# FNet mixing and a dropless mixture of experts: where the first two batches are folded, and which way batch 1 takes to its second stage

## The chip, the cores and the metric

The kernel runs on one core of a Trainium2 chip. The metric is the device time of one execution in microseconds; three executions of the kernel before give a median of 1250.8 us. TensorE (PE) multiplies, VectorE (DVE) and ScalarE (ACT) work elementwise, GpSimd (POOL) here mainly issues indirect DMAs, and SyncE (SP) issues most other DMAs. Every engine works through its own instructions in the order of the program; semaphores tie them together.

## The reference

```python
X = np.fft.fft(x, axis=1)          # x: (8, 2496, 256) float32
X = np.fft.fft(X, axis=2)
x = X.real.reshape(19968, 256)
logits = x @ w_gate                # 8 experts
expert_idx = np.argmax(logits, axis=1)
gate_w = softmax(logits)[row, expert_idx]
for e in range(8):                 # rows of expert e
    h = np.maximum(x_e @ w1[e], 0) # 256 -> 1024
    y_e = h @ w2[e]                # 1024 -> 256
out = gate_w[:, None] * y          # rows in their own order
```

All in float32: 8 batches of 2496 tokens are mixed by a two-dimensional Fourier transform, of which the real part is kept, and every token then goes through one of 8 two-layer networks.

## The kernel before, in words

The sequence of 2496 is split as 104 x 24. A batch goes through these steps.

*First stage.* The batch comes in three loads ("thirds", `load`, tile `xq`, three buffers), each with four sequence columns and their mirror images, 8 x 256 numbers per partition. `fold` adds a column to its mirror image (L321), and `fold_d` folds the feature axis: the sum and the difference of a row and the same row read backwards (L310, L311) and a small copy (L312). The last third has a column of its own that goes to `pm0`. `half1` multiplies two folded columns by a wave table (`con["w1"]`, 112 columns, or `wp`, the same 110 columns in another order) into PSUM, and ACT copies the result to `t1` (L336). In the trace these matmuls are `s<-xq,w`.

*Between the stages* the rows have to change partitions. Batch 0 does this inside SBUF: in `first_whole`, each of its 12 columns is sent by a small DMA from `t1` to its place in `t4s` (L375), which works since `wp` has the columns in the order that makes the target regular. For every other batch `first` writes each third's `t1` to the DRAM tensor `Td` (L411), and `regroup` reads it back, transposed, into `t4s` in two DMAs (L423).

*Second stage* (`second`): for each half of the batch, groups of matmuls (`pr`, `p<-table,t4s`) go to `zz`, then for five windows of 128 tokens two matmuls (`p<-table,zz`) give the transformed rows and the router's logits. ACT copies parts (L475, L478, mirror at L454), VectorE makes two sets of rows (L480), and `route` (L486) picks the expert on VectorE, counts ranks by matmuls (`rk`) and gives every row a place. `waiting` holds ten scatters per half; `send` issues the next one as an indirect DMA on the POOL queue (L540, shown under the helper's line L238), for batches after 0 with a copy on ACT and a cast on POOL ahead of it. `plan` (L548) makes the table of blocks from the counts, some 22 tiny VectorE operations per block size.

*Expert blocks* (`experts`): a block of 512, 256 or 128 rows of one expert is fetched from `Xs` (`fetch_rows`, five SP DMAs), its weights are fetched (`fetch_weights`), `turn` transposes the rows on VectorE (L654) and negates the odd half on ACT (L657), and two layers of matmuls follow (`ph`, `py`). Blocks of 512 use seven products in place of eight, for which `Left` forms weight sums in a scratch tile `ws` (L637). The first rounds have two blocks of 256 and four of 128 from batch 0, then four of 256 from batch 1.

The order of the work is written out by hand with generators. Every `yield` is a step; the bottom of the kernel decides how many steps of one part are taken between those of another, and since all engines work in program order, this fixes what stands ahead of what on each of them. `second(0)` is stepped through with the first stage of batch 1 (`early`) woven in by `PLAN` (which step of `second(0)` is followed by how many of `early`). After it, `experts` drives: it yields its amount of work, and `side` (the next batch's second stage, and the first stage of the one after, `mixed`) is stepped in proportion. Ahead of the first block stand 12 empty yields (L854), each of which takes one step of `side`. In the kernel before, `early`'s last steps, the table of batch 0 (`close(0)`) and `mixed(1)` are woven from there.

Batch 1's three loads are issued at the end of `first_whole`; batch 2's are issued as `first` of batch 1 releases buffers, the last of them behind `regroup` of batch 1 (L1006).

Of the kernel before, what the change touches and what calls it, by code (L numbers as in the profile page):

```python
# [188 lines left out]
PLAN = {3: 1, 5: 1, 7: 1, 11: 1, 12: 1, 13: 2, 14: 1, 15: 1, 16: 1}  # L189
# [28 lines left out]
def kernel(ctx: ExitStack, tc, x, w_gate, w1, w2, out):  # L218
# [88 lines left out]
    def fold_d(o, a, n):  # L307

        lo, hi = free(a, 1, [D, n], [1, H - 1]), free(a, D - 1, [D, n], [-1, H - 1])
        vec.tensor_tensor(free(o, 1, [D, n], [1, H - 1]), lo, hi, op=ALU.add)  # L310
        vec.tensor_tensor(free(o, H + 1, [D, n], [1, H - 1]), lo, hi, op=ALU.subtract)  # L311
        vec.tensor_copy(free(o, 0, [D, n], [H, 2]), free(a, 0, [D, n], [H, 2]))  # L312

    def fold(xq, q, pm0):

        a, m = xq[:, 0:4], xq[:, 4:8]
        n = 4
        if q == NQ - 1:
            n = 3
            fold_d(pm0, m[:, 3], 1)  # L320
        vec.tensor_tensor(a[:, 0:n], a[:, 0:n], m[:, 0:n], op=ALU.add)  # L321
        yield
        fold_d(m, a, 4)
        yield

    def half1(b, q, half, pm, pm0, t1):
        ps = pm_.tile([NP, 2, D], F32, tag="m", name="s1")
        for i in range(2):
            s = 4 * q + 2 * half + i
            if s < NS - 1:  # L330
                mm(ps[:, i], con["w1"][:, s], pm[:, 2 * half + i])
                continue
            for k, lo, hi in ((NS - 1, 0, H + 1), (NS + 1, H + 1, D)):
                mm(ps[:, i, lo:hi], con["w1"][:, k], pm0[:, lo:hi], True, False)
                mm(ps[:, i, lo:hi], con["w1"][:, k + 1], pm[:, 3, lo:hi], False, True)
        act.copy(t1[:, 2 * half:2 * half + 2], ps[:])  # L336
# [80 lines left out]

    base = con["cap"]
# [9 lines left out]
    t4s = cp.tile([128, 2 * HALF, D], F32, name="t4s")  # L428
    zz = cp.tile([128, 2, NW * 128], F32, name="zz")
# [118 lines left out]
    def plan(b, size, k, last):  # L548
# [38 lines left out]
        if not last:  # L587

            vec.tensor_scalar(n[:], ex[:], -1.0, float(k), op0=ALU.mult, op1=ALU.add)
            vec.scalar_tensor_tensor(n[:], n[:], 0.0, nb[:], op0=ALU.max, op1=ALU.min)  # L590
            nxt = one("gone", E)
            vec.scalar_tensor_tensor(nxt[:], n[:], float(size), gone[:], op0=ALU.mult, op1=ALU.add)
            gone = nxt
        yield
        tabs[b, size, last] = tab
# [27 lines left out]
    class Left:  # L623


        def __init__(self, w1_sb):
            ws = bp.tile([128, 3, F // 2], F32, tag="ws", name="ws", bufs=2)
            o = [ws[:, k] for k in range(3)]
            a11, a12, a21, a22 = (w1_sb[:, c, k * F // 2:(k + 1) * F // 2] for k in range(2) for c in range(2))
            self.all = a11, a12, o[2], a22, o[0], o[1], a21  # L630
            self.due = deque([(o[0], a21, a22, add), (o[1], o[0], a11, sub), (a21, a11, a21, sub),
                              (o[2], a12, o[1], sub)])
# [167 lines left out]
    def experts(todo):  # L800
# [44 lines left out]
        for k, (b, size, last, at) in enumerate(todo):  # L845
            n, m = size // 128, BIG // size
            if not k:
# [3 lines left out]
                while b not in whole:  # L851
                    yield 0, True
                fetch_some(0)
                for _ in range(12):  # L854
                    yield 0, False
# [144 lines left out]
    def ahead_of(b):  # L1000

        yield from first(b)
        regroup(b, 0)
        regroup(b, 1)
        if b == 1:
            load(b + 1, NQ - 1)  # L1006

    def mixed(b):

        one, two = (ahead_of(b + 1) if b + 1 < B else iter(())), second(b)  # L1010
        for _ in range(3):
            next(one, None)
            yield
        for k, _ in enumerate(two):
            if k % 2 == 0:
                next(one, None)
# [41 lines left out]
    for _ in range(3):  # L1058
        next(early)
    for k, _ in enumerate(second(0)):  # L1060
        for _ in range(PLAN.get(k, 0)):
            next(early, None)
        send()
    work = experts(todo)
    steps = {b: mixed(b) for b in range(1, B)}
    for b in range(1, B):
# [4 lines left out]
        if b == 1:  # L1071
            side = woven(chain(close(0), through(0)), chain(early, side))
# [77 lines left out]
```

## Time and profile before

| | |
|---|---|
| three runs | 1249.64, 1250.80, 1251.31 us; median 1250.8 us |
| profiled execution | 1254.3 us; span from first to last instruction 1252.5 us, mean granted TensorE clock 0.977 |
| busy share | PE 97%, PEld 87%, DVE 63%, ACT 35%, POOL 36% |
| chain that ended last | PE 83%, DVE 8%, DMA 3%, ACT 2%, issue 2% |
| DMA | 248.35 MB, mean 198 GB/s |

A busy share is an average over the whole span. The page also gives it in 40 slices of 31.3 us: TensorE has 7, 7, 6 tenths in the first three and 9 in nearly all others, and the granted TensorE clock is 0.7, 0.7, 0.6 there and 0.9 or more afterwards. All that the diff touches happens in the first 140 us, so the trace is read there, in short stretches. Times below are microseconds from the start of the span.

### The profile page before, as it was taken

The page shows a single profiled execution, that of the slowest core. Times are in us where ns is not written, and L with a number is a line of the kernel's source. Part 1 is how long each engine was busy: PE and PEld are TensorE (multiplying, and loading weights), DVE is VectorE, ACT ScalarE, POOL GpSimd, SP SyncE. Part 2 cuts the span into 40 slices and gives each one's busy share as a digit, 9 for nine tenths or more (in the row PEclk, how much of TensorE's full clock was granted, in tenths as well). Part 3 has the DMA queues.
Part 4 walks back from the last instruction along what each step waited for, and adds up shares of the span by engine and source line. Part 5 has one row for each costly group of instructions (what it writes and reads, how often), then busy time and mean ns, then how long its engine had stood idle before and what let it go on. Part 6 is the DMA issues. An engine that isn't in the chain of part 4 may idle for free.

```text
span 1252.5 us, 22624 instructions
## 1 busy us (share of the span) xinstructions
PE 1209.7 (97%) x7389; PEld 1094.7 (87%) x7389; DVE 786.0 (63%) x1862; ACT 441.7 (35%) x1186; POOL 451.8 (36%) x531
## 2 busy tenths in 40 slices
PE   7769999999999999999999999999999999999997
PEld 5558888888888899889988899889989999999996
DVE  4655334566556787666865588686888884444663
ACT  2433333344443433434343433432332332222222
POOL 0336327155137321571226612571463241111112
PEclk7769999999999999999999999999999999999999
DMA  8579899865648443663337434443436238788887
GB/s 242 179 249 348 284 312 310 227 184 193 169 148 266 120 160 117 195 215 112 102 129 216 142 115 165 135 156 97 130 131 190 94 112 305 269 280 289 284 274 283
DMA packets 163065, 248.35 MB, mean 198 GB/s; under 512 B 118542, under 2 KB 130200, under 8 KB 143473
## 3 DMA queue, kind: packets, MB, share of 16 engines
q1 hardware_dynamic: 145644, 201.79, 50.5%
q0 software_dynamic: 16080, 42.85, 9.5%
q10 hardware_dynamic: 1221, 2.24, 0.5%
q8 instruction: 60, 0.98, 0.3%
q14 instruction: 60, 0.49, 0.1%
HBM read 193.45 MB, written 53.45 MB: 197 GB/s over the span
## 4 chain that ended last, share of the span: by engine, by line
PE 83%; DVE 8%; DMA 3%; ACT 2%; issue 2%; SPq 0%; POOL 0%; POOLq 0%; DVEq 0%; ACTq 0%
PE py L223 24%; PE a L223 12%; PE c L223 11%; PE ph L223 9%; PE b L223 6%; PE p L223 6%; PE d L223 6%; PE e L223 5%; PE s L223 4%; DMA xq<-in_x_dram 2%; DVE xT L654 1%; DVE y L754 1%; DVE hT L709 1%; DVE hT L712 1%; DVE hT L706 1%
## 5 line engine op out<-in xcount | busy, mean ns | idle before, releaser
L238 POOL DMA_INDIRECT out_dram<-y,ro x163 | 162.1, 995 | 627.5 <-ACT y L750 303.4
L223 PE MATMUL py<-w_sb,hT 128*128 128x256 f32 x1504 | 340.8, 380 | 0.4 <-DVE hT L908 0.4
L223 PEld LDWEIGHTS py<-w_sb,hT 128*128 128x128 f32 x1504 | 281.1, 190 | 36.6 <-DVE hT L908 0.8
L238 POOL DMA_INDIRECT Xs<-rows,pi x160 | 161.2, 1008 | 87.3 <-POOL pi L539 41.8
L223 PE MATMUL ph<-xT,w_sb 128*128 128x128 f32 (+1 forms) x896 | 127.7, 300 | 4.7 <-DVE ro L863 4.7
L223 PE MATMUL a<-xT,w_sb 128*128 128x256 f32 (+1 forms) x560 | 130.3, 359 | 0.3 <-DVE xT L654 0.3
L223 PEld LDWEIGHTS ph<-xT,w_sb 128*128 128x128 f32 x896 | 118.8, 193 | 11.1 <-DVE ro L863 5.1
L480 DVE SCALAR_TENSOR_TENSOR rows<-p,zs 128x129 f32<-128x129 f32 x160 | 48.8, 347 | 126.0 <-ACT lg L478 125.4
L223 PEld LDWEIGHTS a<-xT,w_sb 128*128 128x128 f32 x560 | 97.6, 190 | 11.7 <-DVE xT L654 0.9
L657 ACT ACTIVATE xT<-xT 128x256 f32<-128x256 f32 (+1 forms) x94 | 36.5, 388 | 173.3 <-DVE xT L654 131.5
L962 ACT ACTIVATE y<-py,xb 128x256 f32<-128x256 f32 x94 | 44.6, 474 | 139.1 <-PE py L223 138.9
L706 DVE TENSOR_TENSOR hT<-hT,b 128x512 f32<-128x512 f32 x63 | 43.3, 687 | 77.5 <-PE b L223 50.3
L716 ACT ACTIVATE hT<-a 128x512 f32<-128x512 f32 x63 | 37.6, 597 | 150.3 <-PE a L223 145.7
L908 DVE TENSOR_SCALAR hT<-ph 128x512 f32<-128x512 f32 x31 | 21.4, 690 | 104.1 <-PE ph L223 52.3
L539 POOL CAST pi<-due 128x1 int32<-128x1 f32 x140 | 47.3, 338 | 64.9 <-ACT due L538 64.9
L223 PE MATMUL c<-xT,ws 128*128 128x256 f32 (+1 forms) x280 | 66.4, 364 | 0.9 <-DVE hT L712 0.2
L223 PE MATMUL a<-w_sb,hT 128*128 128x128 f32 x528 | 66.0, 276 | 0.0
L223 PE MATMUL b<-xs,ws 128*128 128x256 f32 (+1 forms) x280 | 65.0, 359 | 0.0
L223 PE MATMUL d<-xT,w_sb 128*128 128x256 f32 (+1 forms) x280 | 64.9, 358 | 0.0
L223 PE MATMUL e<-xs,w_sb 128*128 128x256 f32 (+1 forms) x280 | 64.9, 358 | 0.0
L223 PE MATMUL c<-xs,ws 128*128 128x256 f32 (+1 forms) x280 | 64.9, 358 | 0.0
L223 PEld LDWEIGHTS a<-w_sb,hT 128*128 128x128 f32 x528 | 63.1, 192 | 0.7
(163 smaller groups left out, 2123.7 us busy)
## 6 DMA issues: line engine op xcount, KB each, us to landing
w_sb<-in_moe_w_dram SPq DMA_DIRECT2D x132, 1024.0 KB
xq<-in_x_dram SPq DMA_DIRECT2D x23, 896.0 KB
xb<-Xs SPq DMA_DIRECT2D x112, 128.0 KB
Td<-t SPq DMA_DIRECT2D x18, 448.0 KB
t4s<-Td SPq DMA_DIRECT2D x7, 768.0 KB
t4s<-Td SPq DMA_DIRECT2D x7, 640.0 KB
xb<-Xs SPq DMA_DIRECT2D x52, 64.0 KB
xb<-Xs SPq DMA_DIRECT2D x88, 32.0 KB
```

The costliest lines, as they stand in the source:

```text
L223: nc.tensor.matmul(o, lhsT=lhsT, rhs=rhs, start=start, stop=stop, **kw)
L238: return unordered(pool.indirect_dma_start(out=dst, out_offset=bass.IndirectOffsetOnAxis(ap=idx, axis=0), in_=rows, in_offset=None, bounds ...
L480: vec.scalar_tensor_tensor(rows[:, k + m, 0:NY], p3[:, 0:NY], zs[:, 0:1], zs[:, 1:], op0=ALU.add, op1=op)
L539: pool.tensor_copy(idx, due[:])
L654: vec.transpose(free(xT[:], 256 * h, [32, n // 32], [BIG, 2], [1, 32]), free(xb, 512 * h, [64, n // 32], [1, 2], [2, 32]))
L657: act.activation(odd, odd, ACTF.Copy, scale=-1.0)
L706: vec.tensor_tensor(h12, h11, b[:], op=add)
L709: vec.tensor_tensor(h21, h12, d[:], op=add)
L712: vec.tensor_tensor(h22, h21, c[:], op=add)
L716: act.activation(h11, a[:], ACTF.Relu)
L908: vec.tensor_scalar(o, ph[:], 0.0, None, op0=ALU.max)
L962: act.activation(y[:, i % 2], py[:], ACTF.Copy, scale=meta[:, i, 1:2])
```

## The change

Batch 1 gets a first stage of its own (`first_one`). Thirds 0 and 1 are folded on GpSimd, both at once at its first step; third 2 is folded on VectorE in pieces of two columns. It multiplies by `wp` instead of `con["w1"]`, VectorE instead of ACT copies the results out of PSUM, and twelve small SP DMAs bring them to `t4b` inside SBUF, as for batch 0. `t4b` is a view of a new tile `spare`, which `Left` later uses, two halves in turn, in place of its two `ws` buffers. There is no `Td[1]` and no `regroup` for batch 1.

Batch 2 (`first_two`) has all three thirds folded on GpSimd in its first step; its products, ACT copies and the way through `Td` stay. The load of its last third is issued in `experts`, behind the row fetch of the first block. The other batches keep `first`.

The order changes: `PLAN` is a new table; all of `early` is issued before `experts` begins, after the first four steps of `close(0)`; a table counts as known one step earlier (`tabs[...]` ahead of the `yield` in `plan`); 14 empty yields stand ahead of the first block instead of 12; `mixed(1)` takes one step of batch 2's first stage first and no other before step 8 of `second(1)`. In the built program this puts one group of batch 2's first-stage matmuls ahead of block 0's first layer, where there were three, and block 0's first two groups of `ph` stand side by side.

The diff:

```diff
--- before.py
+++ after.py
@@ -186,7 +186,7 @@
 SHARE, EARLY, ROOM = 0.6, 0.7, 1.2
 AHEAD = 12
 WARM = 44
-PLAN = {3: 1, 5: 1, 7: 1, 11: 1, 12: 1, 13: 2, 14: 1, 15: 1, 16: 1}
+PLAN = {7: 2, 11: 1, 12: 2, 13: 2, 14: 1, 15: 1, 16: 1, 17: 1}
 MOST = max(k for now in rounds() for _, k, _ in now)
 
 
@@ -304,36 +304,42 @@
                     in_=x[row:row + NP].rearrange("p (c j d) -> p c j d", c=2, d=D)[:, :, 2 * k:2 * k + 2])
                 yield
 
-    def fold_d(o, a, n):
+    def fold_d(o, a, n, eng=vec):
 
         lo, hi = free(a, 1, [D, n], [1, H - 1]), free(a, D - 1, [D, n], [-1, H - 1])
-        vec.tensor_tensor(free(o, 1, [D, n], [1, H - 1]), lo, hi, op=ALU.add)
-        vec.tensor_tensor(free(o, H + 1, [D, n], [1, H - 1]), lo, hi, op=ALU.subtract)
-        vec.tensor_copy(free(o, 0, [D, n], [H, 2]), free(a, 0, [D, n], [H, 2]))
-
-    def fold(xq, q, pm0):
+        eng.tensor_tensor(free(o, 1, [D, n], [1, H - 1]), lo, hi, op=ALU.add)
+        eng.tensor_tensor(free(o, H + 1, [D, n], [1, H - 1]), lo, hi, op=ALU.subtract)
+        eng.tensor_copy(free(o, 0, [D, n], [H, 2]), free(a, 0, [D, n], [H, 2]))
+
+    def fold(xq, q, pm0, eng=vec):
 
         a, m = xq[:, 0:4], xq[:, 4:8]
         n = 4
         if q == NQ - 1:
             n = 3
-            fold_d(pm0, m[:, 3], 1)
-        vec.tensor_tensor(a[:, 0:n], a[:, 0:n], m[:, 0:n], op=ALU.add)
-        yield
-        fold_d(m, a, 4)
+            fold_d(pm0, m[:, 3], 1, eng)
+        eng.tensor_tensor(a[:, 0:n], a[:, 0:n], m[:, 0:n], op=ALU.add)
+        yield
+        fold_d(m, a, 4, eng)
         yield
 
     def half1(b, q, half, pm, pm0, t1):
         ps = pm_.tile([NP, 2, D], F32, tag="m", name="s1")
+        n = NR if b == 1 else NP
+        col = (lambda s: wp[:, s]) if b == 1 else (lambda s: con["w1"][:, s])
         for i in range(2):
             s = 4 * q + 2 * half + i
+            o = ps[0:n, i]
             if s < NS - 1:
-                mm(ps[:, i], con["w1"][:, s], pm[:, 2 * half + i])
+                mm(o, col(s), pm[:, 2 * half + i])
                 continue
             for k, lo, hi in ((NS - 1, 0, H + 1), (NS + 1, H + 1, D)):
-                mm(ps[:, i, lo:hi], con["w1"][:, k], pm0[:, lo:hi], True, False)
-                mm(ps[:, i, lo:hi], con["w1"][:, k + 1], pm[:, 3, lo:hi], False, True)
-        act.copy(t1[:, 2 * half:2 * half + 2], ps[:])
+                mm(o[:, lo:hi], col(k), pm0[:, lo:hi], True, False)
+                mm(o[:, lo:hi], col(k + 1), pm[:, 3, lo:hi], False, True)
+        if b == 1:
+            vec.tensor_copy(t1[0:n, 2 * half:2 * half + 2], ps[0:n])
+        else:
+            act.copy(t1[0:n, 2 * half:2 * half + 2], ps[0:n])
 
     ahead = {}
 
@@ -415,6 +421,66 @@
             pm = xq[:, 4:8]
             yield
 
+    def first_one():
+
+        pm0 = xp.tile([NA, D], F32, tag="pm0", name="pm0")
+
+        def folds(q, eng=vec):
+            xq = ahead[1, q]
+            a, m = xq[:, 0:4], xq[:, 4:8]
+            n = 4
+            if q == NQ - 1:
+                n = 3
+                fold_d(pm0[:], m[:, 3], 1, eng)
+                yield
+            for lo in (0, 2):
+                eng.tensor_tensor(a[:, lo:min(n, lo + 2)], a[:, lo:min(n, lo + 2)], m[:, lo:min(n, lo + 2)], op=ALU.add)
+                yield
+            for lo in (0, 2):
+                fold_d(m[:, lo:lo + 2], a[:, lo:lo + 2], 2, eng)
+                yield
+
+        def products(q):
+            pm = ahead.pop((1, q))[:, 4:8]
+            t1 = xp.tile([NP, 4, D], F32, tag="t1", name="t1")
+            for half in range(2):
+                half1(1, q, half, pm, pm0, t1)
+                for i in range(2):
+                    s = 4 * q + 2 * half + i
+                    nc.sync.dma_start(out=t4b[s:GP:NS, 0:NG], in_=t1[0:NR, 2 * half + i])
+                if half and q < NQ - 1:
+                    load(2, q)
+                yield
+
+        for q in range(2):
+            for _ in folds(q, pool):
+                pass
+        yield
+        yield from products(0)
+        yield from woven(folds(2), products(1))
+        yield from products(2)
+        for h in range(2):
+            ahead[1, "t4", h] = t4b[:, h * HALF:(h + 1) * HALF]
+
+    def first_two():
+
+        pm0 = xp.tile([NA, D], F32, tag="pm0", name="pm0")
+        pms = []
+        for q in range(NQ):
+            xq = ahead.pop((2, q))
+            for _ in fold(xq, q, pm0[:], pool):
+                pass
+            pms.append(xq[:, 4:8])
+        yield
+        for q in range(NQ):
+            t1 = xp.tile([NP, 4, D], F32, tag="t1", name="t1")
+            half1(2, q, 0, pms[q], pm0, t1)
+            yield
+            half1(2, q, 1, pms[q], pm0, t1)
+            nc.sync.dma_start(out=Td[2][:, 4 * q * D:4 * (q + 1) * D], in_=t1[:].rearrange("p j d -> p (j d)"))
+            load(3, q)
+            yield
+
     base = con["cap"]
 
     def regroup(b, h):
@@ -426,6 +492,9 @@
         ahead[b, "t4", h] = t4
 
     t4s = cp.tile([128, 2 * HALF, D], F32, name="t4s")
+    spare = cp.tile([128, 2, 3, F // 2], F32, name="spare")
+    t4b = spare[:].rearrange("p a b f -> p (a b f)").rearrange("p (g d) -> p g d", d=D)
+    turns = [0]
     zz = cp.tile([128, 2, NW * 128], F32, name="zz")
 
     def second(b):
@@ -591,8 +660,8 @@
             nxt = one("gone", E)
             vec.scalar_tensor_tensor(nxt[:], n[:], float(size), gone[:], op0=ALU.mult, op1=ALU.add)
             gone = nxt
-        yield
         tabs[b, size, last] = tab
+        yield
 
     def fetch_rows(b, size, tab, i, flat=None):
 
@@ -624,7 +693,8 @@
 
 
         def __init__(self, w1_sb):
-            ws = bp.tile([128, 3, F // 2], F32, tag="ws", name="ws", bufs=2)
+            ws = spare[:, turns[0] % 2]
+            turns[0] += 1
             o = [ws[:, k] for k in range(3)]
             a11, a12, a21, a22 = (w1_sb[:, c, k * F // 2:(k + 1) * F // 2] for k in range(2) for c in range(2))
             self.all = a11, a12, o[2], a22, o[0], o[1], a21
@@ -850,8 +920,10 @@
                 fetch_some(0, 1)
                 while b not in whole:
                     yield 0, True
+                fetch_some(0, 1)
+                load(2, NQ - 1)
                 fetch_some(0)
-                for _ in range(12):
+                for _ in range(14):
                     yield 0, False
                 for xT in turn(b, size, xbs[0][0]):
                     pass
@@ -999,20 +1071,21 @@
 
     def ahead_of(b):
 
-        yield from first(b)
+        if b == 1:
+            yield from first_one()
+            return
+        yield from first_two() if b == 2 else first(b)
         regroup(b, 0)
         regroup(b, 1)
-        if b == 1:
-            load(b + 1, NQ - 1)
 
     def mixed(b):
 
         one, two = (ahead_of(b + 1) if b + 1 < B else iter(())), second(b)
-        for _ in range(3):
+        for _ in range(1 if b == 1 else 3):
             next(one, None)
             yield
         for k, _ in enumerate(two):
-            if k % 2 == 0:
+            if k % 2 == 0 and (b > 1 or k > 7):
                 next(one, None)
             yield
         yield from woven(close(b), one)
@@ -1055,12 +1128,16 @@
         else:
             vec.tensor_copy(con["rd"][:, c, to + E:to + 2 * E], pg[:])
     early = ahead_of(1)
-    for _ in range(3):
-        next(early)
+    next(early)
     for k, _ in enumerate(second(0)):
         for _ in range(PLAN.get(k, 0)):
             next(early, None)
         send()
+    closed = close(0)
+    for _ in range(4):
+        next(closed)
+    for _ in early:
+        send()
     work = experts(todo)
     steps = {b: mixed(b) for b in range(1, B)}
     for b in range(1, B):
@@ -1069,7 +1146,7 @@
         side = chain(steps[b], islice(steps.get(b + 1, iter(())), AHEAD))
         ticks = TICKS + AHEAD * (b == 1)
         if b == 1:
-            side = woven(chain(close(0), through(0)), chain(early, side))
+            side = woven(chain(closed, through(0)), side)
         blocks = [(size, k * size / BIG, halved(b - 1, size)) for size, k, _ in rounds()[b - 1]]
         total = sum(k * (15 if seven_ else 16) for _, k, seven_ in blocks)
         open_ = sum(k * (8 if seven_ else 16) for _, k, seven_ in blocks)
```

More of the change, by code (lines that the diff above doesn't have):

```diff
@@ L593, in plan @@
             gone = nxt
+        tabs[b, size, last] = tab
         yield
-        tabs[b, size, last] = tab
     def fetch_rows(b, size, tab, i, flat=None):
```

## The prediction

> **What bounds the kernel now.** I read four views in turn: the busy shares, then the stretches of 5 us for the place where TensorE is idle, then the waits for the reason, then the timeline for the chain behind it. TensorE is 97% busy, so of the span's 1252.5 us only 42.8 are without a matmul, and the slices put most of that ahead of 110 us. Columns below: stretch, length, busy us (and instructions) of PE, PEld, DVE, ACT, POOL, then granted clock, DMA share, GB/s.
>
> ```profile
> 55.00:60.00 5.00, 2.15 (x23) 1.67 (x21) 3.84 (x20) 1.98 (x7) 2.79 (x3) 0.86 0.93 313
> 60.00:65.00 5.00, 0.00 (x0) 0.00 (x0) 4.62 (x23) 0.00 (x0) 3.59 (x3) 0.50 0.61 206
> 65.00:70.00 5.00, 0.43 (x3) 0.47 (x3) 4.66 (x19) 0.00 (x0) 3.78 (x5) 0.50 0.99 314
> 70.00:75.00 5.00, 5.00 (x20) 4.56 (x21) 0.31 (x5) 1.83 (x5) 3.81 (x4) 0.50 1.00 350
> ...
> 80.00:85.00 5.00, 2.83 (x16) 2.12 (x16) 3.69 (x14) 2.63 (x11) 0.00 (x0) 1.00 0.32 68
> 85.00:90.00 5.00, 2.26 (x5) 1.85 (x6) 3.21 (x14) 0.74 (x3) 0.00 (x0) 0.59 0.45 99
> ```
>
> Two holes stand out: 58 to 69.5, and 82 to 87.7. After each the clock is at 0.50 for some microseconds, so work there takes twice as long. The waits up to 120 us name them:
>
> ```profile
> PE pr L223 <- DMA t4s<-Td: 11.2, 1, 11.2
> PE ph L223 <- DVE ro L863: 4.7, 1, 4.7
> ```
> ```profile
> SPq L606 <- DMA Xs<-rows,pi: 12.6, 2, 11.6
> ```
>
> The first is batch 1's trip through DRAM (Td written, read back as t4s). The second is the start of the first expert block, and behind it SyncE waited 11.6 us for batch 0's scattered rows. The timeline gives that chain:
>
> ```profile
> 73.75 0.97 POOL L238 DMA_INDIRECT Xs<-rows,pi  x1 [0.30 <-issue]
> ...
> 81.15 1.96 SPq L606 DMA_DIRECT2D xb<-Xs  x4
> ...
> 86.99 0.70 DVE L654 STREAM_TRANSPOSE xT<-xb 128x512 f32<-128x512 f32 x1
> ...
> 87.74 3.78 PE L223 MATMUL ph<-xT,w_sb 128*128 128x256 f32 x8 [4.68 <-DVE ro L863]
> ...
> 113.14 7.07 PE L223 MATMUL ph<-xT,w_sb 128*128 128x256 f32 x32
> ```
>
> Read it as: last row scatter issued at 73.75, landed 7.4 us later, fetched, transposed, block 0 at 87.74. That, not the hole of 11.2 us, is the clock of the start: a matmul brought forward into the hole helps only if it would otherwise stand behind block 0.
>
> **A yardstick.** In both programs TensorE has the same matmuls ahead of block 1's first layer, which starts at 113.14, and soon after it the instruction orders agree. So I sum to that point.
>
> **The change, part by part.**
>
> *GpSimd folds two thirds of batch 1.* A fold is an add of 1024 elements per partition, an add and a subtract of 508, and a copy. GpSimd's nearest row is the weight differences:
>
> ```profile
> L678 POOL TENSOR_TENSOR ws<-w_sb,ws x26: 1269/1302/1616, 413.6 to 1010.7; 128x512 f32<-128x512 f32 x26
> ```
>
> 512 elements in 1.30 us is 2.54 ns each: 2.6 + 2 x 1.3 + 0.6 for the copies (the casts at L539 are 0.34) gives 6.0 us per third. No row has GpSimd reading backwards as these folds do, so 5.5 to 9 us; I take 6.0. Third 0 lands at 29.3 (there L321 starts), so it is done at 35.3, third 1 at 41.3; the row scatters queued behind them on POOL start at 44.96 today. Hidden, then, up to 7.8 us a third. VectorE loses two folds (1.22 + 0.69 + 0.68 + 0.17 us each) and L321's wait for the second load, about a window of rows earlier; but the two matmul groups and VectorE's copies of them now stand together ahead of the routing (about 3 us).
>
> Here a rule weighs against the change. The trace shows VectorE held by GpSimd:
>
> ```profile
> 410.77 1.46 POOL L678 TENSOR_TENSOR ws<-w_sb 128x512 f32<-128x512 f32 x1
> ```
> ```profile
> 411.13 1.64 DVE L310 TENSOR_TENSOR xq<-xq 104x508 f32<-104x508 f32 x1
> 412.70 0.67 DVE L311 TENSOR_TENSOR xq<-xq 104x508 f32<-104x508 f32 x1
> ```
>
> L310 takes 1.64 us instead of 0.67, ending 0.54 after GpSimd's add. The Trainium skill (SBUF — State Buffer, section Who interferes with whom) generalises: a VectorE instruction with two SBUF inputs is blocked for the whole of a GpSimd instruction that reads SBUF. By the row alone, which shows it on long operands, routing's small operations lose nothing and the one-hot of half 0 is ready at 41.0; by the rule its five two-input operations (L495, L496, L498, L501, L505) each wait 0.3 to 0.5 us and it is ready at 42.8. Today it is 42.04. I take 42.0: no change.
>
> *VectorE copies batch 1's first stage (ACT did).* Half 1 of batch 0 today takes from 42.04 to 60.10 (`base`). VectorE gets four copies at 0.69 (L908, PSUM to SBUF, 128x512) = 2.8 us and the cut-up third 2 (two 0.42 pairs for each 0.68 pair). TensorE paces the middle of this stretch at clock 0.50, so some is covered; what is not: a fold between the last rows and the reduce (1.2) and two copies between the one-hot and `base` (1.4). Price 2.5, `base` at 62.6. If TensorE stays at full clock here it is 3 us less.
>
> *Sends.* Ten scatters follow. Today their nine gaps average 1.44 us; the ones near VectorE's fold of batch 2 are 1.8 to 1.95, the rest 1.28. That fold leaves VectorE: 62.6 + 0.7 + 9 x 1.28 = 74.8 for the last issue, +1.1.
>
> *Batch 1 inside SBUF, third 2 of batch 2 behind the rows.* Td's write and read-back, 1.3 MB each way, become twelve SBUF copies of 110 KB (0.77 us of SyncE each, none of it late: the last pair trails the last VectorE copy as batch 0's do, 4 us from copy to L223's `pr`, so batch 1 resumes at 65 instead of 69.56). A 0.9 MB load goes behind the first rows. What this buys is the landing. Two stretches, 44 to 48 and 71 to 75 us:
>
> ```profile
> Xs<-rows,pi POOLq DMA_INDIRECT x2, 3.2
> ```
> ```profile
> Xs<-rows,pi POOLq DMA_INDIRECT x3, 7.4
> ```
>
> 7.4 us is at a DMA share of 1.00; 3.2 to 7.4 bound it. Only 2 MB of weights now share the way, so 4.0: rows landed at 78.8 (81.15). The fetch moved its last bytes 3.9 us after issue today (the DMA engines fall idle at 85.0), and VectorE's folds hid that until 86.99; now the rows can be transposed at 82.8.
>
> *GpSimd folds all of batch 2.* It starts when the last scatter has been issued, 75.8. Third 0 takes 5.5, and routing of batch 1, at that time on VectorE, costs it 0.9 more: 82.2. In TensorE's order batch 2's first matmul group stands between batch 1's half and block 0: 1.9 us at clock 0.50, 84.1. In ACT's order its copy (0.59) stands ahead of the odd half of xT (0.42): 85.1 against today's 88.14. So block 0 starts 3.0 earlier, bound by GpSimd and no longer by the rows. Thirds 1 and 2 are done at about 88 and 95, needed at about 94 and 101: hidden, 6 us in hand. Batch 1's scatters wait behind them (95 instead of 97.8 by program order: nothing).
>
> *Moved behind block 0.* Today three groups of batch 2's first stage run before block 0, then one: 2 x 0.95 = 1.9 us comes behind it. VectorE's routing, held by the folds, may stop `p` once: 0.4 (0 to 1.5).
>
> *Fourteen ticks, scratch tile moved, table known earlier.* They set the order counted above; no cost of their own. Left's scratch (L637) is first needed at 239 us.
>
> Sum: -3.0 + 1.9 + 0.4 = -0.7 us. The profiled execution has 1254.3 us (1252.5 and 1.8 around it), 3.5 over the median 1250.8; a difference carries over: **1250.1 us**. This kernel's measurement can tell about 0.2% (2.5 us) from no change.
>
> **Rivals.**
>
> *A, likeliest, 0.45: the gain of the landing is paid back* as summed. Own range -3 to +2.
>
> *B, 0.30: faster, 1246.8.* The routing isn't held (one-hot at 41.0) or TensorE keeps its clock in half 1. For it: the stretch from 30 to 35 has clock 0.88, and fewer stalls on VectorE keep TensorE denser; against: 0.50 from 40 on. One of them is 1 to 3 us on the whole chain; with 2 us and a landing of 3.4, rows and folds are ready 2.6 earlier: -0.7 - 2.6 = -3.3, with -4 taken for some of both.
>
> *C, 0.20: slower, 1254.9: GpSimd becomes the bound.* At 9 us a third, batch 1's third 0 is done at 38.3, and VectorE's copy of its product, ahead of the routing in VectorE's queue, moves the one-hot by 2; the last scatter's end is 77.8; the fold of batch 2 ends 9 later at 86.8, plus 1.9 and 1.0: 89.7 against 88.14, +1.6, and 1.9 + 0.6 moved behind: +4.1. It decides from about 8.2 us a third. For it: backward reading, the lock. Against: the rows at 1.30.
>
> *D, 0.05: the trip inside SBUF is no shorter* (twelve small copies land late): batch 1's half stays where it was, routing reaches VectorE at 84 and delays xT; about +0.5, 1251.3.
>
> **How the numbers follow.** A reaches 2.5 us to either side only at its ends (0.03 faster, 0.04 slower). Faster: nearly all of B, 0.29, and A's end: 0.32. Slower: C and A's end, 0.24. Same: 0.44. The range holds B's centre and most of its far side (1246.0, a clock kept through half 1) and C's centre less its tail: 1246.0 to 1254.9.
>
> **What would show it.** Right: `pr` of batch 1 near 65; last scatter issued near 74.8 and landed in 4; the first fold group of batch 2 on POOL ending near 82, ph at 84 to 85, and block 1's first layer 112 to 113. Half 1's clock at 0.50. Wrong: folds on POOL above 8 us a third; `s` or ph waiting for POOL; routing's short operations at 1 us and more; block 1 before 110 or after 116.

## The result, and the profile after

The changed kernel takes 1246.91 us (median of 15 runs, 1244.42 to 1250.88) where the kernel before takes 1250.38 us on the same chip (15 runs, 1248.34 to 1255.59). The ratio is 0.9971, with a 95% interval of 0.9959 to 0.9982: faster by about 3.5 us. The forecast was 1250.1 us and "the gain of the landing is paid back". Two later measurements, on two chips, gave 0.9966 (0.9957 to 0.9974) and 0.9973 (0.9961 to 0.9985). On one more chip, of which more below, nothing of the gain was left.

A caution before the lines are read: the two profiled executions differ by more than the medians. That of the kernel before (1254.3 us) was 3.9 over its median, that of the changed kernel (1244.87 us, span 1243.1) 2.0 under its own.

First the same stretches of 5 us (length, busy us and instructions of PE, PEld, DVE, ACT, POOL, granted clock, DMA share, GB/s), changed kernel:

```profile
45.00:50.00 5.00, 4.97 (x28) 4.06 (x26) 3.44 (x8) 2.11 (x10) 3.88 (x4) 0.90 0.36 110
...
55.00:60.00 5.00, 1.41 (x16) 1.26 (x14) 3.79 (x22) 0.27 (x1) 1.96 (x2) 0.50 0.75 237
60.00:65.00 5.00, 2.24 (x11) 2.27 (x11) 4.35 (x29) 0.53 (x2) 3.91 (x4) 0.50 0.65 216
...
70.00:75.00 5.00, 1.71 (x12) 1.49 (x12) 3.18 (x9) 2.15 (x10) 4.60 (x4) 1.00 0.43 161
75.00:80.00 5.00, 2.72 (x6) 1.66 (x7) 3.18 (x7) 1.00 (x2) 4.92 (x5) 0.68 0.58 136
```

Both holes of TensorE are still there and earlier. The first is shorter. The second is as long as before (4.8 us); a group of batch 2 and 0.7 us more of waiting follow it. The DMA share between 70 and 75 us, where the last rows of batch 0 have to land, is 0.43 instead of 1.00. The waits up to 120 us of the same kernel:

```profile
PE pr L223 <- DVE p_nb L630: 6.3, 1, 6.3
PE s L223 <- POOL xq L312: 4.8, 1, 4.8
PE ph L223 <- DVE xT L724: 0.7, 1, 0.7
```
```profile
SPq L675 <- DMA Xs<-rows,pi: 10.0, 1, 10.0
```

`pr` waits 6.3 us instead of 11.2. The name behind the arrow misleads: `pr` reads nothing of the table of blocks, and other profiles of this kernel name other tiny instructions of that table. In the trace TensorE's queue first goes through the counters of its DMA queues, which hold it until 62.65, and looks at VectorE's last. What it waits for are the last small DMAs into `spare`, issued up to 57.54; the last of their completions is counted at 62.41. In front of block 0 TensorE's wait (4.7 us for `ro` before) now stands at the first group of batch 2, which waits 4.8 us for GpSimd. Then the chain that set the start, in the timeline:

```profile
70.46 0.98 POOL L238 DMA_INDIRECT Xs<-rows,pi  x1 [0.30 <-issue]
...
74.32 2.38 SPq L675 DMA_DIRECT2D xb<-Xs  x4
...
78.40 0.71 DVE L724 STREAM_TRANSPOSE xT<-xb 128x512 f32<-128x512 f32 x1 [1.73 <-DMA xb<-Xs]
...
79.17 5.89 PE L223 MATMUL ph<-xT,w_sb 128*128 128x256 f32 x16 [0.71 <-DVE xT L724]
...
106.12 7.07 PE L223 MATMUL ph<-xT,w_sb 128*128 128x256 f32 x32
```

The last scatter is issued at 70.46 (73.75 before), the fetch starts 3.9 us later (7.4 before), and VectorE waits 1.73 us for the fetched rows: in this profile block 0 hangs on its rows, with nothing of VectorE's in between. (In two later profiles of the same kernel something of VectorE's does stand there; see "GpSimd sets block 0" below.) Block 1 starts at 106.12 instead of 113.14.

### The profile page after: what moved, and what is told of

Same layout as the page of the kernel before. It is cut to its first block, busy times and chain, and to the rows that moved or that the text cites. A ratio compares the mean times of both kernels' runs of the same rounds, so it can differ in the third digit from the quotient of the medians.

```text
span 1243.1 us, 22669 instructions
## 1 busy us (share of the span) xinstructions
PE 1205.0 (97%) x7389; PEld 1092.3 (88%) x7389; DVE 784.7 (63%) x1849; ACT 438.0 (35%) x1180; POOL 475.0 (38%) x562
## 4 chain that ended last, share of the span: by engine, by line
PE 68%; issue 18%; DVE 8%; POOL 3%; ACT 2%; DMA 1%; POOLq 0%; SPq 0%; DVEq 0%; ACTq 0%
PE py L223 20%; PE a L223 10%; PE c L223 9%; PE p L223 6%; PE b L223 5%; PE d L223 5%; PE ph L223 5%; PE e L223 4%; PE s L223 3%; POOL out_dram L238 3%; DVE xT L724 1%; DVE y L824 1%; ACT y L820 1%; DVE hT L776 1%; DVE hT L779 1%
## 5 line engine op out<-in xcount | busy, mean ns | idle before, releaser
L223 PE MATMUL c<-xT,spare 128*128 128x256 f32 (+1 forms) x280 | 66.5, 364 | 0.9
L223 PE MATMUL c<-xs,spare 128*128 128x256 f32 (+1 forms) x280 | 64.9, 358 | 0.0
L223 PE MATMUL b<-xs,spare 128*128 128x256 f32 (+1 forms) x280 | 64.9, 359 | 0.0
```

Of the source, the lines that this page charges most:

```text
L223: nc.tensor.matmul(o, lhsT=lhsT, rhs=rhs, start=start, stop=stop, **kw)
```

## The experiments

### Three parts of the change taken back, one at a time

(The four runs on a second chip, which stand last here, came before these.)

*Batch 1 through DRAM again*, the folds and copies as changed:

```diff
-        n = NR if b == 1 else NP
-        col = (lambda s: wp[:, s]) if b == 1 else (lambda s: con["w1"][:, s])
+        n = NP
+        col = lambda s: con["w1"][:, s]
...
-                    nc.sync.dma_start(out=t4b[s:GP:NS, 0:NG], in_=t1[0:NR, 2 * half + i])
+                if half:
+                    nc.sync.dma_start(out=Td[1][:, 4 * q * D:4 * (q + 1) * D], in_=t1[:].rearrange("p j d -> p (j d)"))
...
-            ahead[1, "t4", h] = t4b[:, h * HALF:(h + 1) * HALF]
+        regroup(1, 0)
+        regroup(1, 1)
```

> Batch 1's first stage goes through DRAM and back as before; the folds on GpSimd, VectorE's copies, the late load and the 14 steps stay. Theory 'landing' (the gain comes from the traffic that no longer stands beside batch 0's last rows): 3 to 4 us over the changed kernel, so level with the kernel before or 1 us over it; the last scatter lands 5 to 7.5 us after its issue instead of 3.9, and batch 1's first resampling product starts at 66 to 70 us instead of 62.8. Theory 'folds' (the gain is VectorE's relief from five folds): within 1 us of the changed kernel, 0.997 of the kernel before.

*Thirds 0 and 1 of batch 1 folded on VectorE again*, the trip inside SBUF and the rest as changed:

```diff
-PLAN = {7: 2, 11: 1, 12: 2, 13: 2, 14: 1, 15: 1, 16: 1, 17: 1}
+PLAN = {3: 1, 7: 2, 11: 1, 12: 2, 13: 2, 14: 1, 15: 1, 16: 1, 17: 1}
...
-            for _ in folds(q, pool):
+            for _ in folds(q):
                 pass
-        yield
+            yield
```

> Thirds 0 and 1 of batch 1 are folded on VectorE, one of them in step 3 of batch 0's second half and one in step 7; the trip inside SBUF, the rest on GpSimd and all else stay. Theory 'landing': within 1 us of the changed kernel in the end; the first routing one-hot comes at 41.5 to 43 us instead of 40.1, and no operation of the first routing is held by GpSimd (0.24 us each instead of 1.2 to 1.5 for three of them). Theory 'folds': 1.5 to 3 us over the changed kernel, the whole of batch 0's rows later by that much. If GpSimd's holding of VectorE costs more than the folds do (three operations by 1.1 us): 1 us under the changed kernel.

*Thirds 0 and 1 of batch 2 folded on VectorE again*:

```diff
-            for _ in fold(xq, q, pm0[:], pool):
+            for _ in fold(xq, q, pm0[:], pool if q == NQ - 1 else vec):
```

> Thirds 0 and 1 of batch 2 are folded on VectorE as before, third 2 on GpSimd; all else as in the changed kernel. Theory 'landing': within 1 us of the changed kernel: the first group of batch 2 starts before 76 us because VectorE folds a third in 2.8 us instead of GpSimd's 5.1, but the rows set the start of block 0 anyway. Theory 'folds': 1.5 to 3 us over the changed kernel, since VectorE has 5.5 us of folds more at the time when it does batch 1's routing and block 0's transposes. Rival C of the prediction (GpSimd is the bound at block 0): 1 to 2 us under the changed kernel.

Beside them, on the same chip, the changed kernel itself:

> The changed kernel itself, beside the three partial undoings, so that all share one chip. On the chip of the prediction it was 0.9971 of the kernel before; on a second chip 1.0009. There TensorE's completion signals came late in bursts (none before 409.04 to 414.60 us, then four within 0.2 us) and TensorE stood idle for 35.6 us after 56 us instead of 14.8. If the size of the gain depends on such stalls, a chip without them (span about 1243 to 1247) gives 0.996 to 0.998, and one with them (span about 1275 to 1280) gives 0.999 to 1.002. If the gain is the same everywhere, 0.9971 again.

| | median us | ratio to the kernel before (95%) |
|---|---|---|
| kernel before | 1251.81 | |
| changed kernel | 1247.11 | 0.9966 (0.9957 to 0.9974) |
| batch 1 through DRAM | 1251.35 | 1.0002 (0.9990 to 1.0014) |
| batch 1 folded on VectorE | 1252.47 | 1.0014 (1.0001 to 1.0026) |
| batch 2 folded on VectorE | 1248.13 | 0.9978 (0.9966 to 0.9989) |

The gain is there again. Taking back the trip inside SBUF gives up 4.2 us, all of the gain within the interval. So far "landing" is right and "folds" wrong. But taking back GpSimd's folds of batch 1 gives up 5.4 us, which is more than the whole change brought and which neither theory allowed: "landing" had put it at under 1 us. Taking back the two folds of batch 2 gives up 1.0 us, with overlapping intervals, so that they are worth anything is not shown; "GpSimd is the bound at block 0" would have made that variant faster.

The profiles say where each loses. With batch 1 through DRAM, the waits from 60 us on:

```profile
PE pr L223 <- DMA t4s<-Td: 13.9, 2, 12.1
PE ph L223 <- DVE ro L934: 4.3, 1, 4.3
```

and in its timeline:

```profile
69.24 0.98 POOL L238 DMA_INDIRECT Xs<-rows,pi  x1 [0.30 <-issue]
...
75.73 1.92 SPq L674 DMA_DIRECT2D xb<-Xs  x4
```

The scatter is out even earlier than in the changed kernel, and the fetch follows 6.5 us later instead of 3.9. The landing is slow again as soon as the traffic of `Td` is back. The direction is clear, the size less so. In this profile landing and fetch take 3.3 us longer than in the mean of the changed kernel's three profiles (table below), but both halves are shorter (half 1 takes 16.5 us instead of 17.6, at a granted clock of 0.90), and counted from the first `pr` block 1 starts only 1.1 us later. The profiled execution lay 1.5 us under its own median. That the trip is worth 4.2 us is shown by the medians; this one profile locates only a part of it.

With batch 1 folded on VectorE, VectorE's own timeline of batch 0's first half reads:

```profile
29.21 1.29 DVE L437 TENSOR_TENSOR xq<-xq 104x512 f32<-104x512 f32 x2 [3.41 <-DMA xq<-in_x_dram]
...
34.33 1.29 DVE L437 TENSOR_TENSOR xq<-xq 104x512 f32<-104x512 f32 x2 [1.83 <-DMA xq<-in_x_dram]
...
37.02 0.61 DVE L549 SCALAR_TENSOR_TENSOR rows<-p,zs 128x129 f32<-128x129 f32 x2
...
42.91 1.28 DVE L340 COPY t<-s 110x512 f32<-110x512 f32 x2
...
45.40 0.24 DVE L570 TENSOR_TENSOR oh<-table,v 128x80 bf16<-128x80 f32 x1
```

VectorE stands still 3.41 and 1.83 us for loads of batch 1, then folds, and batch 0's rows and routing wait behind in its queue; two copies more stand right ahead of the routing. The one-hot comes 19.1 us after batch 0's first `pr` instead of 14.4 to 15.2. The kernel before has the same two waits in the same place, without the copies:

```profile
29.32 1.22 DVE L321 TENSOR_TENSOR xq<-xq 104x1024 f32<-104x1024 f32 x1 [4.67 <-DMA xq<-in_x_dram]
...
33.96 1.23 DVE L321 TENSOR_TENSOR xq<-xq 104x1024 f32<-104x1024 f32 x1 [1.50 <-DMA xq<-in_x_dram]
...
35.10 0.60 DVE L480 SCALAR_TENSOR_TENSOR rows<-p,zs 128x129 f32<-128x129 f32 x2
```

So the parts don't add up one by one: the two losses, 4.2 and 5.4 us, together are twice the gain. With the folds on VectorE, batch 0's first half is 3.5 us longer than in the kernel before (19.1 against 15.9 and 15.3), about what the landing gives. The two copies are 1.3 us of it. Another part comes from the order of this variant: it folds the whole second third in one go, so the next rows start at 37.02, where the kernel before lets them through after the first addition, at 35.10. A variant that folds on VectorE in the old order was not run, so how much of the 5.4 us belongs to GpSimd as such is open. With the folds on GpSimd that half is shorter than before. By the medians, neither of the two parts brought anything here without the other.

### The kernel before once more, and batch 2's trip

> The kernel before, profiled a second time. If the first profile was typical: from batch 0's first resampling product to its first one-hot 16.2 us, to the last scatter's issue 47.9, to block 1 87.3. If the first profile was a late one (it stood 3.9 us over its own median), the last scatter is issued at 45 to 47 us from that product, and block 1 starts at 83 to 86. VectorE's first fold of batch 1 waits some 6 us for the load of third 1, with the routing of half 0 behind it in the queue.

> The changed kernel itself, as the base for the two variants beside it: 0.9966 of the kernel before, give or take 0.001, on a chip on which TensorE's completion signals are not late. Counted from batch 0's first resampling product, so that the loads at the start are left out, its profile has block 0 at 53.5 to 54.5 us and the start of block 1 at 80.5 to 82.5; the wait for batch 2's trip through DRAM in front of its resampling is between 0 and 3 us.

The changed kernel took 1247.01 us beside 1251.03 for the kernel before (0.9973, 0.9961 to 0.9985). The second profile of the kernel before has its last scatter at 46.1 us after the first `pr`, and block 1 at 85.1: so the first one (47.9 and 87.3) was a late one, as its distance from the median said. With two profiles of the kernel before and three of the changed kernel the span can be cut at rows of the timeline, each piece set beside the forecast's term. All are starts of rows: first `pr` of batch 0; `oh` of half 0; `base` of half 1; the tenth scatter of half 1; the first fetch of rows; `ph` of block 0; `ph` of block 1.

| piece | before, us | changed, us | change of the means | forecast |
|---|---|---|---|---|
| start to the first `pr` | 25.9, 26.3 | 25.5, 28.3, 26.0 | +0.5 | 0 |
| half 0, to its one-hot | 15.9, 15.3 | 14.4, 15.2, 14.4 | -0.9 | 0 |
| half 1, to `base` | 18.1, 17.1 | 18.1, 17.3, 17.3 | 0.0 | +2.5 |
| to the last scatter | 13.8, 13.8 | 12.4, 12.4, 12.4 | -1.4 | -1.4 |
| landing, to the fetch | 7.4, 6.8 | 3.9, 4.0, 3.7 | -3.3 | -3.4 |
| fetch to block 0 | 6.6, 6.6 | 4.8, 5.4, 5.7 | -1.3 | -0.7 |
| block 0 to block 1 | 25.4, 25.6 | 27.0, 27.8, 26.2 | +1.5 | +2.3 |
| block 1 to the end | 1139.4, 1139.7 | 1137.0, 1140.7, 1141.2 | +0.1 | 0 |
| sum | 1252.5, 1251.2 | 1243.1, 1251.1, 1246.8 | -4.8 | -0.7 |

-4.8 is near the -3.5, -4.7 and -4.0 by which the medians fell. Of the 4.1 us between the two sums, half 1 alone makes 2.5. The first and the last row show what one profile is worth: they vary by 3 and 4 us without a cause in the change. The landing and the sends stand far outside that; half 0's 0.9 is only just clear of its spread.

In the second and third profile of the changed kernel, and in the variant with batch 2 folded on VectorE, something had come up behind block 1. This is a wait of the latter:

```profile
PE pr L223 <- DMA t4s<-Td: 3.0, 1, 3.0
```

(1.4 and 2.0 us in the two profiles of the changed kernel.) Batch 2 still takes the way through DRAM, and block 1 now comes to it sooner. Two variants bring that trip forward, the first by the order of steps alone, the second with the VectorE folds as well:

```diff
-            if k % 2 == 0 and (b > 1 or k > 7):
+            if (b > 1 and k % 2 == 0) or (b == 1 and (k == 8 or k > 10)):
```

> Batch 2's first stage takes its steps one after another from step 11 of batch 1's half instead of at every second one, so that its last third's products come ahead of block 0's second layer instead of behind it. Theory 'paid back at batch 2's trip' (after block 1 has moved forward, TensorE waits 1.4 us, in a variant 3.0 us, for the read-back of batch 2, and runs at a lower clock after it): the wait goes, and the time falls by 1.5 to 3 us under the changed kernel. Theory 'the wait is chance' (the changed kernel's first profile had none): within 0.7 us. If the earlier trip collides with block 1's rows or its weights: 1 to 2 us slower.

> The same order of steps, and batch 2's thirds 0 and 1 folded on VectorE. By 'paid back at batch 2's trip' this takes away the 3.0 us wait that stood in the profile of the variant with these two folds on VectorE: level with the variant of the steps alone or 1 us under it, 2 to 4 under the changed kernel. If VectorE is the bound around block 0 (routing of batch 1, folds, transposes): 1 to 2 us over the changed kernel.

In both profiles the wait is gone. The times are 1246.05 us (0.9951, 0.9935 to 0.9968, only five runs) and 1247.80 us (0.9972, 0.9963 to 0.9981), beside 1247.01 for the changed kernel. The first may be a microsecond or two better, but its interval overlaps the changed kernel's, and the second, with the same wait removed, is level. Whether batch 2's trip costs anything is therefore open. That the wait exists is shown, that it is worth 1.5 us or more is not.

### Four kernels on a second chip

These came first, and all on one chip that runs this program slower: the kernel before at 1278.39 us.

> The changed kernel itself once more, for a second look and as the base of the three beside it. Its profile had block 1's first layer at 106.1 us (113.1 before), 7.0 us earlier, and the span 9.4 us shorter, while the medians differ by 3.5. If those 7 us belong to the change, block 1 starts at 106 to 107 again and the ratio is 0.997. If a good part is the state of TensorE's clock in half 1 of batch 0 (0.90 between 45 and 50 us there, 0.50 before) and that state falls out by chance, block 1 starts somewhere between 106 and 110, with a lower clock in that stretch when it is late.

> Undoes one part: ScalarE copies batch 1's first-stage results out of PSUM instead of VectorE. By the prediction's price (2.5 us for VectorE's copies between one-hot and base) base of half 1 comes 1.4 to 2.5 us earlier, and with it the scatters and block 0: 1 to 2 us under the changed kernel (1245). Rival: ScalarE's copies (0.59 each, six) delay the small copies that the rows and the routing wait for, base is no earlier or later, 0 to 2 us over.

> Undoes one part: the load of batch 2's last third is issued at the end of batch 1's first stage, ahead of the weights and the rows, as before. Theory of the landing: the last scatters share the DMA engines again and land after about 7 us instead of 3.9, block 0 starts 3 us later, 2 to 3 us over the changed kernel (1249 to 1250). Rival, the load is hidden anyway: landing 4 to 5 us, the same time as the changed kernel within 1 us; or a little faster, since GpSimd's last fold no longer waits for it.

> Adds 96 bfloat16 matmuls of 128x256 whose result nobody reads into TensorE's three waits: 24 ahead of the rank counts of batch 0's half 0, 36 ahead of batch 1's second stage, 36 ahead of batch 2's first group. Clock theory: half 1 of batch 0, batch 1's second stage and block 0's first two groups run at clock 1.00 instead of 0.50; the rank counts to base of half 1 gain up to 2 us, block 0's first groups 2.9: 2 to 4 us under the changed kernel (1243 to 1245). Rival, VectorE and the scatters pace the stretch: only the 1.9 of block 0's first groups, or nothing. If 24 run at half clock they end after the one-hot and cost up to 1 us.

The edits, in the same order (the first is the changed kernel as it is; in the last, `heat` issues bf16 products of constants into PSUM banks that are free then, 96 in three places, and nothing is left out of the computation):

```diff
-            vec.tensor_copy(t1[0:n, 2 * half:2 * half + 2], ps[0:n])
+            act.copy(t1[0:n, 2 * half:2 * half + 2], ps[0:n])
```
```diff
         yield from products(2)
+        load(2, NQ - 1)
         for h in range(2):
...
-                fetch_some(0, 1)
-                load(2, NQ - 1)
                 fetch_some(0)
```
```diff
+        if b == 0 and h == 0:
+            heat(24)
         rk = pm_.tile([128, NSL + 1, E], F32, tag="m", name="rk")
...
+            if b == 1 and h == 0:
+                heat(36)
...
+            if q == 0:
+                heat(36)
             half1(2, q, 0, pms[q], pm0, t1)
```

| | median us | ratio to the kernel before (95%) |
|---|---|---|
| changed kernel | 1279.27 | 1.0009 (0.9989 to 1.0028) |
| ScalarE copies batch 1's first stage | 1280.99 | 1.0017 (0.9994 to 1.0039) |
| batch 2's last third loaded early | 1284.69 | 1.0060 (1.0040 to 1.0081) |
| products in TensorE's waits | 1283.62 | 1.0041 (1.0022 to 1.0061) |

*Copies.* With the copies back on ScalarE, half 1 (one-hot to `base`) takes 20.5 us, as it does with them on VectorE (20.5). Half 0 is 0.9 shorter. No gain came of it in the time. So the forecast's 2.5 us for VectorE's copies in half 1 isn't there. This run tests that term directly, though on this chip alone.

*Load.* Loading batch 2's last third ahead of the rows costs 5.4 us here, more than the 2 to 3 expected; landing and the way from the fetch to the transpose are 1.1 and 2.5 us longer in its profile. In the trace the four row transfers that the transpose needs are complete at 83.5, and it starts at 90.8, straight behind batch 1's routing on VectorE. So the early load's cost is shown for this chip, but only a part of it is the landing.

*Clock.* The time went the other way, 4.4 us over the changed kernel. Three stretches of the kernel with the extra products:

```profile
40.00:45.00 5.00, 4.84 (x42) 4.09 (x40) 3.99 (x19) 2.33 (x9) 1.52 (x2) 1.00 0.81 243
45.00:50.00 5.00, 2.90 (x20) 2.41 (x18) 2.25 (x6) 0.94 (x4) 3.78 (x5) 1.00 0.53 155
50.00:55.00 5.00, 2.05 (x4) 1.06 (x4) 1.36 (x5) 1.24 (x6) 3.78 (x5) 0.50 0.92 271
```

The clocks without them are 0.68, 0.98 and 0.71. Over the whole of half 1 the mean granted clock rose only from 0.71 to 0.76, and half 1 became 21.6 us instead of 20.5. At block 0 the products stand in the way (the transpose starts 3.5 us before `ph` instead of 0.8). What the clock is worth can't be read from this run, since ScalarE stands still for 3.15 us in its half 1, from 47 to 50, for a late signal of the kind that the next paragraph describes. The ten profiles from the other three chips say more. There half 1 takes 18.1, 18.1 and 18.4 us at a mean clock of 0.69, from 16.8 to 17.6 at 0.79 to 0.81 (five profiles), and 16.3 and 16.5 at 0.89 and 0.90. So half 1's length does go with TensorE's clock. Whether the clock shortens half 1, or a half with fewer waits keeps the clock up, no run here separates.

*The chip.* The changed kernel's profile there has TensorE idle for 35.6 us from 56 us on, counting only gaps over 0.4 us, where the first chip has 14.8. Some of this idleness stands where TensorE, VectorE and ScalarE all stand still:

```profile
70.10 0.77 PE L223 MATMUL p<-table,zz 128*128 128x145 f32 x4 [1.47 <-issue]
...
75.42 0.27 ACT L544 COPY zs<-p 128x130 f32<-128x130 f32 x1 [5.37 <-remote]
75.79 0.61 DVE L549 SCALAR_TENSOR_TENSOR rows<-p,zs 128x129 f32<-128x129 f32 x2 [5.94 <-remote]
```

ScalarE needs nothing but this product; it ends at 70.9, and ScalarE starts 4.5 us later. In the trace TensorE's semaphore, which ScalarE waits for, is not counted up between 69.67 and 75.39. From 409.04 to 414.60 us the same happens while five groups of products end, and then four counts come within 0.2 us. Neither the kernel before nor the changed one shows a burst of this kind on the first chip, and no kernel does on the two later ones. In the first of these gaps batch 1's routing stood still, so the rows of block 0, landed in 4.0 us as elsewhere, had their transpose 8.8 us after the start of the fetch instead of 4.1 to 4.9. That is some 4 us at the very place where the change gains. Why the signals are late on that chip is not known, and the kernel before was not profiled there, so it isn't shown that they take just this gain.

## Why the prediction was wrong in its likeliest case

Its range held the time, and its point was 3.2 us too high. Point by point:

*What bounds the start: right in the main.* The chain from the last scatter over landing and fetch to block 0 set the start in all three profiles of the changed kernel on the faster chips; in two of them VectorE's routing added up to 0.9 us behind the landed rows (below). The landing went from 7.1 to 3.9 us (forecast 4.0). Batch 1 through DRAM brought a landing of 6.5 us and the old time back. The sends, 1.28 us apart without VectorE's fold, were right to 0.1.

*"Half 1: price 2.5": the step that failed most.* It charged VectorE 2.8 us of copies and cut-up folds, and counted as covered only what TensorE's slow clock would hide. Here is half 1 before and after, with the same columns as above, and in each VectorE's wait for ScalarE's logits (`lg`) ahead of the rows (ten of them: busy us and mean ns, then the idle time ahead of them):

```profile
42.04:60.10 18.06, 14.34 (x80) 12.35 (x79) 10.57 (x44) 7.59 (x26) 10.70 (x10) 0.69 0.69 208
L480 DVE SCALAR_TENSOR_TENSOR rows<-p,zs 128x129 f32<-128x129 f32 x10 | 3.0, 347 | 6.6 <-ACT lg L478 6.6
```
```profile
40.14:58.20 18.06, 14.16 (x80) 12.28 (x80) 13.05 (x52) 5.22 (x21) 10.43 (x10) 0.69 0.68 204
L549 DVE SCALAR_TENSOR_TENSOR rows<-p,zs 128x129 f32<-128x129 f32 x10 | 3.0, 348 | 3.2 <-ACT lg L547 3.2
```

VectorE did get busier there (10.6 to 13.1 us of 18.1), but it had been idle for 7.5 us of half 1, 6.6 of them in that wait. The added work went into it: the wait fell to 3.2 us, and half 1 kept its length. The clock isn't behind that: it is 0.69 in both, and in the two kernels' profiles with a clock of 0.80 the lengths are 17.1 before and 17.3 after. An engine's added busy time was taken for time on the chain, without looking at what it waited for there.

*"Half 0: no change": sized wrong by 0.9.* The forecast set VectorE's two products' copies against the two folds and the wait for the second load. The lines above show both loads' waits in VectorE's queue, with batch 0's rows behind them. Of the waits it named only the second load's. Without the first one too, batch 0's first rows start 4.4 us after the first `pr` instead of 6.0 (first profiles). How much of the 0.9 us each item makes is not shown. The rule that the forecast weighed here held: the Trainium skill (SBUF — State Buffer, section Who interferes with whom) has VectorE's two-input instruction blocked for a whole GpSimd instruction, and two short ones in the changed kernel show it:

```profile
37.34 0.54 DVE L564 TENSOR_TENSOR eq<-lg,mx 128x80 f32<-128x80 f32 x1
37.92 1.47 DVE L565 TENSOR_TENSOR eq<-eq,table 128x80 f32<-128x80 f32 x1
```

They take 0.24 us each in the kernel before and in the variant whose folds are on VectorE; L565 stays held through two of GpSimd's instructions and ends when GpSimd's last piece of the third does (39.4). In the three profiles this cost 0.8 to 1.5 us in front of the one-hot, less than the 1.8 that lay between the forecast's two sums. The row alone, which said that short operations lose nothing, was wrong, though its figure (41.0) was the nearer one: counted from the same first `pr` as the kernel before, the one-hots are ready at 40.5 to 41.4. Two errors met.

*"GpSimd sets block 0": its own fold was sized too long by 1.3 us, and it delays block 0 by another way.* The forecast had 6.4 us for the fold of batch 2's first third with routing's hold. Here it is in the timeline of the changed kernel, with routing's held instruction among its own:

```profile
71.45 2.36 POOL L321 TENSOR_TENSOR xq<-xq 104x1024 f32<-104x1024 f32 x1
...
73.90 1.26 POOL L310 TENSOR_TENSOR xq<-xq 104x508 f32<-104x508 f32 x1
73.96 1.29 DVE L565 TENSOR_TENSOR eq<-eq,table 128x80 f32<-128x80 f32 x1
...
75.11 1.26 POOL L311 TENSOR_TENSOR xq<-xq 104x508 f32<-104x508 f32 x1
...
76.57 1.89 PE L223 MATMUL s<-xq,w 104*112 104x256 f32 x4 [4.77 <-POOL xq L312]
```

It took 5.1 us. VectorE is held, GpSimd is not. The first group ends just as the transpose of the rows starts (78.4), so here the rows bound block 0, in a near tie. In the other two profiles of the changed kernel it is VectorE. This is the third:

```profile
76.10 2.33 POOL L321 TENSOR_TENSOR xq<-xq 104x1024 f32<-104x1024 f32 x1
```
```profile
76.38 2.08 DVE L567 TENSOR_TENSOR v<-v,table 128x10 f32<-128x10 f32 x1
...
78.68 0.71 DVE L724 STREAM_TRANSPOSE xT<-xb 128x512 f32<-128x512 f32 x1
```

L567, an operation of 10 elements that takes 0.17 us in the kernel before (L498 there), ends only when GpSimd's addition for the second third of batch 2 does, and the transpose stands behind it in VectorE's queue. The trace has the rows complete at 77.8, 0.9 us before the transpose starts; in the second profile L567 takes 2.08 us too, and the transpose starts 0.7 us after the rows are complete. So GpSimd's folds do reach block 0, through routing on VectorE and not through TensorE's group as forecast. With the two folds on VectorE the hold is gone from the profile, and the time was no better.

The price per element (2.3 to 2.5 ns) and the reading backwards were no problem: rival C, from 8.2 us a third, was far off. The forecast's own terms for batch 1's third add up to 5.8 us, not the 6.0 that it took; 5.5 was measured.

*"1.9 and 0.4 come behind block 0": near*, 1.5 measured for 2.3.

*"4 us from copy to `pr`": too short.* In the changed kernel's first profile it is 6.1 (copy ending at 56.68, `pr` at 62.76). It isn't on the chain, so nothing came of it.

*Rival B* gave 1246.8, the measured figure within 0.1, for reasons that don't hold: the routing is held, and half 1's mean clock in the three profiles of the changed kernel (0.69, 0.80, 0.80) is what the kernel before has (0.69, 0.80). The right number came from the wrong mechanism: it was luck.

## What to carry to other kernels

Before an engine's added work is charged to a chain, look in the same stretch at what that engine waits for: work put into a wait can be free, as here in half 1, while an instruction that waits for a load delays everything queued behind it. Parts of a change that share one engine's queue can't be priced one by one, and taking back one of them can cost more than the whole change brought. Where one profile differs from its own median by as much as the effect, compare several, piece by piece, from a landmark behind the start.

## What the runs showed that I had not expected

The same program took 1247 us in three measurements and 1279 on another chip, whose traces show TensorE's completion counts arriving up to 4.7 us late and in bursts; no bursts were seen on the others. GpSimd's folds hold VectorE's operations of 80 elements to 1.29 and 1.47 us instead of 0.24, and one of 10 elements to 2.08 instead of 0.17. Between 71 and 76 us GpSimd itself loses nothing by it. And the length of half 1 went with TensorE's granted clock, from 18.4 us at 0.69 to 16.3 at 0.89, in both kernels and all variants on three chips, with the direction of cause open.
